# Four query loads begun by two DMA queues in place of one, in an attention kernel on one core

## The chip, the cores and the metric

The kernel runs on one core of a Trainium2 chip. The metric is the device time of one execution in microseconds (us); most runs of one kernel agree within 0.2 us. Times of kernels that were compared were taken on the same chip, in turns.

## The reference

```python
B, H, Sq, Skv, Dh = 8, 16, 16, 2048, 256      # all bfloat16, normal values times 0.05
def reference(q, k, v):
    scores = jnp.einsum('bhqd,bhkd->bhqk', q, k) * q.shape[-1] ** -0.5
    return jnp.einsum('bhqk,bhkd->bhqd', softmax(scores, axis=-1), v)
```

There are 128 heads. K and V are 134 MB each and are read once; Q is 1 MB. The inputs are so small that all softmax weights are nearly equal. The correctness check cannot tell a wrong order of the query heads.

## The kernel before

A job `J(engine, class, emit, deps, dma)` is one instruction or a few; an engine runs its jobs in the order in which they were made. SyncE ("sp") begins all loads, so they stand in one queue.

```python
ku = k.rearrange("b h s d -> (b h s) d").rearrange("(u p t) d -> u p t d", p=128, t=NT)   # 4 heads each
qx = q.rearrange("b h s d -> (b h s) d").rearrange("(u a s) d -> a u (s d)", a=4, s=SQ)
QR = VB[:, 1, 0:SQ, :].rearrange("p s d -> p (s d)")      # query rows, in V's second buffer

def emit_qload(eng, a):           # 32 heads (every fourth) to 32 partitions, 8 KB each
    return eng.dma_start(QR[32 * a:32 * a + 2 * G, :], qx[a])        # 2 * G is 32
def emit_qt(eng):                 # VectorE, 32x32 blocks
    return eng.transpose(QT[:].bitcast(F32), QR.bitcast(F32))
# ... cut ...
j_q = [J("sp", "ldq", lambda eng, a=a: emit_qload(eng, a), [j_qz], dma=(sem_q, 64)) for a in range(4)]
# ... cut: then K of the first 8 heads in four loads of 2 MB (two halves of two blocks), which wait
# for nothing; the next K loads wait for the transposes ("kt") that free their buffer; then V ...
j_qt[0] = J("dve", "qt", emit_qt, j_q)
```

After that, ScalarE spreads QT into block-diagonal weights QW, VectorE transposes K in 32x32 blocks ("kt", KN to KB), TensorE multiplies, and so on for 16 groups of 8 heads. A block of K holds four heads, one in each quadrant of 32 partitions. So query head 4u+a has to be in quadrant a, which is why the queries come in four loads of 32 partitions.

## Time and profile before

| | before |
|---|---|
| time, median of 6 runs | 639.76 us (639.58 to 639.93) |
| span of the profiled run | 638.1 us |
| bytes moved | 270.62 MB |

The page of the profile of the kernel before, its span and the rate of all DMA engines in 40 equal slices:

```profile
span 638.1 us, 5071 instructions
...
GB/s 312 429 436 429 430 429 442 429 440 427 431 427 431 429 431 431 429 435 438 426 443 427 431 427 431 429 429 433 433 431 438 438 431 427 430 427 431 420 426 265
```

The rate is about 430 GB/s in all slices but the first and the last. The view by windows gives, for stretches from the start of the span, the busy time of each engine (with instructions in brackets), the granted clock, the DMA share and the rate:

```profile
core 0: us, PE busy (x) PEld busy (x) DVE busy (x) ACT busy (x) POOL busy (x), PEclk, DMA share, GB/s
2.00:4.00 2.00, 0.00 (x0) 0.00 (x0) 0.08 (x1) 0.02 (x1) 2.00 (x1) 1.00 1.05 258
4.00:6.00 2.00, 0.00 (x0) 0.00 (x0) 0.00 (x0) 0.00 (x0) 0.92 (x1) 1.00 0.98 217
6.00:8.00 2.00, 0.00 (x0) 0.00 (x0) 0.00 (x0) 0.00 (x0) 0.00 (x0) 1.00 0.99 291
8.00:10.00 2.00, 0.00 (x0) 0.00 (x0) 0.44 (x1) 0.00 (x0) 0.00 (x0) 1.00 1.04 434
200.00:300.00 100.00, 74.55 (x310) 21.74 (x218) 69.16 (x62) 11.62 (x22) 0.00 (x0) 0.90 1.00 432
```

In the middle (200 to 300 us) the 16 DMA engines are busy all the time, at 432 GB/s. From 4 to 6 us they are just as busy (0.98), at half of that, 217 GB/s. A busy DMA engine is not a fast one. The timeline of the start says what was loaded (start, duration, engine, line, operation, and in brackets what ended the idle time before):

```profile
0.74 1.77 SPq L110 DMA_DIRECT2D VB<-in_q_dram  x4
...
2.56 16.47 SPq L212 DMA_DIRECT2D KN<-in_k_dram  x5
9.56 2.31 DVE L113 STREAM_TRANSPOSE QT<-VB 128x2048 f32<-128x2048 f32 x1 [7.48 <-DMA VB<-in_q_dram]
...
14.17 4.50 DVE L128 STREAM_TRANSPOSE KB<-KN 128x2048 f32<-128x2048 f32 x2 [2.30 <-DMA KN<-in_k_dram]
...
18.73 0.61 PE L145 MATMUL S_ps<-KB,QW 128*128 128x512 bf16 x1 [18.73 <-DVE KB L128]
```

The four query issues take 1.77 us of SyncE's time, and K's follow. QT's transpose waits for the queries until 9.56 us, but the first K transpose waits still longer, until 14.17 us. The chain of waits, followed back from the end, is here (start, duration, what):

```profile
605.20 28.28 DMA KN<-in_v_dram
...
633.52 1.93 PE O_ps L178 x16
...
635.55 0.48 DVE O_fin L326
```

The last V loads were begun at 605 us and stood 28 us in a full queue. The kernel is bound by the DMA stream from the start to the tail.

### The profile page before, as it was taken

The page shows a single profiled execution, that of the slowest core. Times are in us where ns is not written, and L with a number is a line of the kernel's source. Part 1 is how long each engine was busy: PE and PEld are TensorE (multiplying, and loading weights), DVE is VectorE, ACT ScalarE, POOL GpSimd, SP SyncE. Part 2 cuts the span into 40 slices and gives each one's busy share as a digit, 9 for nine tenths or more (in the row PEclk, how much of TensorE's full clock was granted, in tenths as well). Part 3 has the DMA queues.
Part 4 walks back from the last instruction along what each step waited for, and adds up shares of the span by engine and source line. Part 5 has one row for each costly group of instructions (what it writes and reads, how often), then busy time and mean ns, then how long its engine had stood idle before and what let it go on. Part 6 is the DMA issues. An engine that isn't in the chain of part 4 may idle for free. (4 is left out here: it accounts for less than half of the span.)

```text
span 638.1 us, 5071 instructions
## 1 busy us (share of the span) xinstructions
PE 490.0 (77%) x2176; PEld 166.1 (26%) x1680; DVE 428.2 (67%) x371; ACT 93.8 (15%) x176; POOL 4.2 (1%) x7
## 2 busy tenths in 40 slices
PE   0748959959499595986959779595995949959897
PEld 0101312314132140321303123131231412214286
DVE  3879494875948569385683957749477594766960
ACT  2030301203021030300303003030120303003010
POOL 2000000000000000000000000000000000000000
PEclk9977987979889798997979979799797989979999
DMA  8999999999999999999999999999999999999996
GB/s 312 429 436 429 430 429 442 429 440 427 431 427 431 429 431 431 429 435 438 426 443 427 431 427 431 429 429 433 433 431 438 438 431 427 430 427 431 420 426 265
DMA packets 13766, 270.62 MB, mean 424 GB/s; under 512 B 1600, under 2 KB 3904, under 8 KB 4416
## 3 DMA queue, kind: packets, MB, share of 16 engines
q1 hardware_dynamic: 13344, 270.36, 99.2%
q10 hardware_dynamic: 416, 0.18, 0.1%
q8 instruction: 4, 0.07, 0.0%
q14 instruction: 2, 0.02, 0.0%
HBM read 269.48 MB, written 1.05 MB: 424 GB/s over the span
## 5 line engine op out<-in xcount | busy, mean ns | idle before, releaser
L145 PE MATMUL S_ps<-KB,QW 128*128 128x512 bf16 x528 | 217.0, 420 | 137.2 <-DMA VB<-in_v_dram 94.1
L128 DVE STREAM_TRANSPOSE KB<-KN 128x2048 f32<-128x2048 f32 x128 | 284.7, 2281 | 55.2 <-DMA KN<-in_k_dram 53.0
L133 PE MATMUL S_ps<-KB,QW 128*128 128x512 bf16 x496 | 207.7, 419 | 0.0
L172 PE MATMUL O_ps<-VB,PT 128*128 128x512 bf16 x896 | 195.6, 379 | 6.8 <-DMA VB<-in_v_dram 6.8
L145 PEld LDWEIGHTS S_ps<-KB,QW 128*128 128x128 bf16 x528 | 54.6, 104 | 345.2 <-issue 282.5
L172 PEld LDWEIGHTS O_ps<-VB,PT 128*128 128x128 bf16 x896 | 86.8, 98 | 118.3 <-issue 15.7
L150 DVE TENSOR_REDUCE negm<-S_ps 128x1 f32<-128x2048 f32 x16 | 36.7, 2292 | 89.2 <-PE S_ps L133 89.2
L154 ACT ACTIVATE P_sb<-S_ps,negm 128x2048 bf16<-128x2048 f32 x16 | 31.5, 1967 | 414.1 <-DVE negm L150 414.1
L158 DVE STREAM_TRANSPOSE PC<-P_sb 128x1024 bf16<-128x1024 bf16 x32 | 37.9, 1222 | 33.8 <-ACT P_sb L154 33.8
L164 DVE COPY PT<-PC 32x1024 bf16<-32x1024 bf16 x128 | 53.5, 418 | 3.4 <-PE O_ps L178 1.7
L122 ACT ACTIVATE QW<-QT 32x128 bf16 (+1 forms) x128 | 54.0, 422 | 11.2 <-DVE QT L113 9.9
L315 ACT ACTIVATE O_tmp<-O_ps,rab 128x256 f32<-128x256 f32 x15 | 7.1, 475 | 93.6 <-issue 93.6
L178 PE MATMUL O_ps<-KN,PT 128*128 128x256 bf16 x128 | 14.6, 273 | 1.1 <-DMA KN<-in_v_dram 1.1
L178 PE MATMUL O_ps<-VB,PT 128*128 128x256 bf16 x128 | 14.1, 273 | 0.4 <-DVE PT L164 0.4
L178 PEld LDWEIGHTS O_ps<-KN,PT 128*128 128x128 bf16 x128 | 12.3, 98 | 3.3 <-issue 1.1
L178 PEld LDWEIGHTS O_ps<-VB,PT 128*128 128x128 bf16 x128 | 12.4, 98 | 2.3 <-DVE PT L164 0.8
L326 DVE TENSOR_SCALAR O_fin<-O_ps,rab 128x256 bf16<-128x256 f32 x2 | 1.0, 484 | 13.0 <-PE O_ps L178 7.2
L320 DVE SCALAR_TENSOR_TENSOR O_fin<-O_ps,rab,O_tmp 128x256 bf16<-128x256 f32 x15 | 6.7, 446 | 1.8 <-issue 1.8
L113 DVE STREAM_TRANSPOSE QT<-VB 128x2048 f32<-128x2048 f32 x1 | 2.3, 2311 | 7.5 <-DMA VB<-in_q_dram 7.5
L297 DVE TENSOR_SCALAR rab<-mask,rinv 128x2 f32<-128x2 f32 x16 | 3.7, 229 | 1.5
L191 POOL MEMSET PT<- 128x4096 f32 x1 | 3.5, 3511 | 0.0
L301 DVE COPY rab<-rab 128x2 f32<-128x2 f32 x15 | 2.5, 167 | 1.2
(11 smaller groups left out, 8.3 us busy)
## 6 DMA issues: line engine op xcount, KB each, us to landing
VB<-in_v_dram SPq DMA_DIRECT2D x28, 4096.0 KB, 23.9
KN<-in_k_dram SPq DMA_DIRECT2D x28, 4096.0 KB, 30.0
KN<-in_k_dram SPq DMA_DIRECT2D x8, 2048.0 KB, 15.0
VB<-in_v_dram SPq DMA_DIRECT2D x4, 2048.0 KB, 17.1
KN<-in_v_dram SPq DMA_DIRECT2D x2, 2048.0 KB, 27.7
KN<-in_v_dram SPq DMA_DIRECT2D x2, 1024.0 KB, 24.3
KN<-in_v_dram SPq DMA_DIRECT2D x3, 512.0 KB, 27.7
VB<-in_q_dram SPq DMA_DIRECT2D x4, 256.0 KB, 5.1
```

Source lines behind the costliest of these rows:

```text
L122: ins = eng.activation(ap_of(dv, dv.offset + 32 * a + e, [[256, 4], [128, 2], [2, 16]]), src.rearrange("p (s b) t -> p b t s", b=4), ACTF. ...
L128: return eng.transpose(KBf[:, c % R_KB].rearrange("p t i -> p (t i)"), KNf[:, e].rearrange("p t i -> p (t i)")[:, n * c:n * c + n])
L133: return eng.add_instruction(mybir.InstMatmult(start_tensor_calc=start, stop_tensor_calc=stop, ldweights=False, tile_size=(128, 128), tile ...
L145: ins = mm(S_ps[:, 2 * h + c, :], QW[:, e, bp, :], rhs, start=(e == 0 and bp == 0), stop=(e == 1 and bp == 7))
L150: return eng.tensor_reduce(out=negm[:], in_=S_ps[:].rearrange("p c n -> p (c n)"), axis=AX.X, op=ALU.max, negate=True)
L154: return eng.activation(P_sb[:], S_ps[:].rearrange("p c n -> p (c n)"), ACTF.Exp, bias=negm[:], scale=1.0, accum_out=lsum[:])
L158: return eng.transpose(PC[:, h].rearrange("p t x -> p (t x)"), P_sb[:, 1024 * h:1024 * h + 1024])
L164: ins = eng.tensor_copy(PT[pr, 32 * h:32 * h + 32, pr], PC[pr, h])
L172: ins = eng.matmul(O_ps[:, 0, :], PT[:, t, :], rhs, start=(t == 0), stop=(t == NT - 1))
L178: ins = eng.matmul(O_ps[:, bank, 0:D], PT[:, t, :], buf[:, t, :], start=(t == 0), stop=(t == NT - 1))
L315: j_ea[g] = J("act", "ea", lambda eng: eng.activation(O_tmp[:], src, ACTF.Copy, scale=rab[:, 0, 0:1]), [("pv", g, 1) if g < last - 1 else ...
L320: j_eb[g] = J("dve", "eb", lambda eng: eng.scalar_tensor_tensor(out=O_fin[:, 0, :], in0=src, scalar=rab[:, 0, 1:2], in1=O_tmp[:], op0=ALU. ...
```

## The change

The intent: the queries of quadrants 0 and 1 are begun by SyncE, those of 2 and 3 by ScalarE, so that each DMA engine has packets of both sorts to choose from.

```diff
-        j_q = [J("sp", "ldq", lambda eng, a=a: emit_qload(eng, a), [j_qz], dma=(sem_q, 64)) for a in range(4)]
+        j_q = [J(("sp", "sp", "act", "act")[a], "ldq", lambda eng, a=a: emit_qload(eng, a), [j_qz], dma=(sem_q, 64)) for a in range(4)]
 # ... cut: two more jobs stand at the head of ScalarE's list, so the loop's indices move by 2 ...
-                 "act": [order["act"][1:3]] + [order["act"][3 * x:3 * x + 3] for x in range(1, last)]}
-        n_tail = {"dve": dve_tail, "pe": 6 * last - 2, "act": 3 * last}
+                 "act": [order["act"][3:5]] + [order["act"][3 * x + 2:3 * x + 5] for x in range(1, last)]}
+        n_tail = {"dve": dve_tail, "pe": 6 * last - 2, "act": 3 * last + 2}
 # ... cut: bookkeeping, "jb.eng == 'sp' or jb.cls == 'st'" becomes "jb.cls in ('ld', 'ldq', 'st')" ...
```

The edit is meant to leave the waits of all engines as they were; both pages count 5071 instructions.

## The prediction

> **What bounds the kernel now.** The DMA stream. The page moves 270.62 MB in a span of 638.1 us (mean 424 GB/s); the view by windows gives a DMA share of 1.00 and 430 to 432 GB/s in every stretch from 18 to 600 us, while TensorE (77%) and VectorE (67%) wait for loads. The chain of waits ends in 28.28 us of "DMA KN<-in_v_dram": the last V loads stand in a full queue. About 431 GB/s over 270.62 MB is 628 us; the rest is start and tail. So DMA time saved at the start should arrive at the end.
>
> **Where the start loses time.** By windows, the stream begins at about 1.5 us, then runs at 180 to 260 GB/s from about 3 to 7.5 us (DMA share near 1.0, so the engines are occupied, not starved), and reaches 410 to 490 GB/s after 8 us. That is the four query loads (256 KB and 32 partitions each). Summing the windows, 2.05 MB have moved by 9.0 us; at 431 GB/s from 1.6 us this would have taken until 6.4 us. So about 2.6 us are lost, and this is the most the change can win. The Trainium skill, "SBUF — State Buffer", section "Door 1: The DMA port swizzle", says that partitions 0 to 63 reach only 8 of 16 DMA ports and 64 to 127 the other 8. The trace agrees in size: about 215 GB/s is half of 431. Loads 0 and 1 share one half, 2 and 3 the other; one queue sends them one after the other.
>
> **What the change does.** Two of the four issues (0.42 us each) move from SyncE to ScalarE, ahead of its table load (1.28 us). ScalarE then waits until 11.90 us for QT anyway, so this is free. SyncE begins its K issues some 0.85 us sooner, worth nothing by itself, since the queue is occupied. Nothing else changes. The gain is that packets for both halves are available to each DMA engine together. If ports were then all used, 1.05 MB would take 2.4 us in place of 4.8 us.
>
> **How much of it.** The same page, section "Can I just issue two DMAs to hit both halves?", reports only +6% for that, and says they serialize: each DMA engine alternates between its two queues, and two engines with the same port in step still block each other. Engines out of step by part of a packet would gain a part. Estimate: gain between 0.3 us (in step) and 2.4 us (all ports), centre 1.4 us, fully on the critical path. QT (9.56 us now) is not critical: K's first transpose waits 2.3 us longer, until 14.17 us.
>
> **Time.** 639.79 - 1.4 = 638.4 us, range 637.2 to 639.7. Faster by over 2% needs 12.8 us, five times the whole loss: 0.5%. Slower by over 2%: 0.5%. Within 2%: 99%.
>
> **What would show it.** Right: GB/s from 2 to 6 us above 260; QT's transpose at 7 to 9 us; the first K transpose at 12 to 13.6 us instead of 14.17; the same shift in the first matmul (18.73 us) and the start of the last V wait; 431 GB/s unchanged in the middle; span shorter by the same amount as the first K transpose is earlier. Wrong: if 2 to 6 us still shows about 215 GB/s, the queues stay in step and nothing is won. If the first K transpose is earlier but the end is not, a stage in the middle was not bound by DMA.
>
> **What would make it wrong.** K rows of the SyncE queue passing ScalarE's query rows, so that QT lands later than K and becomes critical; ScalarE's issues starting late; a mid-kernel stall that absorbs the shift.

## The result

| | before | after |
|---|---|---|
| time, median of 6 runs each | 639.76 us | 639.12 us (638.91 to 639.21) |
| ratio | | 0.999, 95% interval 0.9977 to 1.0003 |
| span of the profiled run | 638.1 us | 637.7 us |
| repeated later (9 and 5 runs) | 639.65 us | 639.06 us |

A ratio is the mean time of one kernel's runs over that of the other's of the same rounds, so it is not quite the ratio of these medians. The interval is wider than the effect. But all six runs after are below all six runs before, and the repetition gives the same difference: 0.64 us, then 0.59 us. I take the change to be worth about 0.6 us. That is 0.1%, and less than half of the predicted 1.4 us.

The page of the changed kernel, the same lines:

```profile
span 637.7 us, 5071 instructions
...
GB/s 311 429 443 428 426 430 440 430 438 434 432 428 432 432 428 432 430 430 430 431 443 438 432 430 429 430 432 432 428 432 430 440 432 430 432 436 430 417 423 274
```

By windows, the same stretches:

```profile
2.00:4.00 2.00, 0.00 (x0) 0.00 (x0) 0.07 (x1) 0.95 (x1) 2.00 (x1) 1.00 0.90 258
4.00:6.00 2.00, 0.00 (x0) 0.00 (x0) 0.00 (x0) 0.00 (x0) 0.91 (x1) 1.00 1.05 246
6.00:8.00 2.00, 0.00 (x0) 0.00 (x0) 0.00 (x0) 0.00 (x0) 0.00 (x0) 1.00 1.01 299
8.00:10.00 2.00, 0.00 (x0) 0.00 (x0) 0.28 (x1) 0.00 (x0) 0.00 (x0) 1.00 1.03 418
200.00:300.00 100.00, 74.69 (x314) 21.81 (x221) 69.00 (x62) 11.60 (x22) 0.00 (x0) 0.90 1.00 432
```

From 4 to 6 us the rate rose from 217 to 246 GB/s, where all ports would have given 430; from 2 to 4 us it did not rise, and from 8 to 10 us it is lower than before. A second profile of the same kernel (the run "The change once more" below) shows a faster start:

```profile
2.00:6.00 4.00, 0.00 (x0) 0.00 (x0) 0.07 (x1) 0.96 (x1) 2.91 (x1) 1.00 1.01 277
4.00:6.00 2.00, 0.00 (x0) 0.00 (x0) 0.00 (x0) 0.00 (x0) 0.91 (x1) 1.00 1.19 291
```

So from 4 to 6 us the two profiles of one kernel (246 and 291 GB/s) lie further apart than the first of them and the kernel before. Over 2 to 6 us it is 238 GB/s before, and 252 and 277 after. The timeline of the first profile's start:

```profile
0.73 0.86 SPq L110 DMA_DIRECT2D VB<-in_q_dram  x2
0.73 0.90 ACTq L110 DMA_DIRECT2D VB<-in_q_dram  x2
...
1.64 17.24 SPq L212 DMA_DIRECT2D KN<-in_k_dram  x5
...
9.72 2.31 DVE L113 STREAM_TRANSPOSE QT<-VB 128x2048 f32<-128x2048 f32 x1 [7.65 <-DMA VB<-in_q_dram]
...
14.01 4.50 DVE L128 STREAM_TRANSPOSE KB<-KN 128x2048 f32<-128x2048 f32 x2 [1.98 <-DMA KN<-in_k_dram]
...
18.58 0.61 PE L145 MATMUL S_ps<-KB,QW 128*128 128x512 bf16 x1 [18.58 <-DVE KB L128]
```

The issues ran side by side, as intended (0.86 and 0.90 us), and K's issues began at 1.64 us in place of 2.56. But QT's transpose began a little later than before (9.72), and the first K transpose 0.16 us earlier (14.01). In the second profile of the same kernel it was 0.49 us earlier (13.68). The end of the chain of waits:

```profile
593.87 30.26 DMA KN<-in_v_dram
624.27 10.79 PE O_ps L178 x96
635.15 0.48 DVE O_fin L326
```

The last wait for V now ends at 624 us; the 96 matmuls after it run without a gap, where by its chain the kernel before still waited for V until 633.5 us.

Why was so little won? The DMA view of the changed kernel shows a part of it. These are four stretches of 0.5 us in order, 3.5 to 5.5 us. q1 is SyncE's queue, q10 is ScalarE's; columns are packets, MB, and the share of the 16 engines' time:

```profile
q10 hardware_dynamic: 15, 0.08, 63.5%
q1 hardware_dynamic: 12, 0.04, 32.3%
...
q1 hardware_dynamic: 23, 0.12, 98.3%
q10 hardware_dynamic: 10, 0.00, 2.0%
...
q1 hardware_dynamic: 10, 0.08, 69.2%
q10 hardware_dynamic: 6, 0.05, 45.1%
...
q10 hardware_dynamic: 12, 0.10, 84.2%
q1 hardware_dynamic: 2, 0.00, 0.4%
```

In the first and the last stretch the engines work mostly for ScalarE's queue, in the second nearly only for SyncE's (98% against 2%). The records of single packets, from which these shares are made, show rows of both queues mixed at 3.1 us (8 and 8 under way), then turns: 15 of SyncE's and none of ScalarE's at 4.4 us, none and 16 at 5.5 us, 16 and none at 6.6 us. So most of the 16 engines turn from one queue to the other together. By theory, while all write quadrants 0 and 1 the ports of the other half have nothing to do, and the other way round, and this keeps the gain small. The turns are seen in the trace; this consequence is argued, and the packets support it only weakly. Rows that had 4 to 7 others of their own queue beside them, and as many of the other queue, still took 463 ns; those with 10 or more of their own took 527 (second profile: 448 and 460).

The packets also give the size. A query row of 8 KB took 563 ns on average before; after, 521 on SyncE's queue and 504 on ScalarE's (493 over both in the second profile). In the wide load below the mean is 363 ns and the median 309. So the change took away some 50 to 70 of 200 ns, and with 8 rows for each engine that is 0.4 to 0.6 us. About half of it was lost again on K's rows of 16 KB: those begun before 17 us took 645 ns on average before, 657 and 663 in the two profiles after, and 611 in the kernel with the wide load. With 268 rows over 16 engines this is 0.2 to 0.3 us.

### The profile page after: what moved, and what is told of

Its sections match the earlier page's. It is cut to its first block, busy times and chain, and to the rows that moved or that the text cites. A ratio compares the mean times of both kernels' runs of the same rounds, so it can differ in the third digit from the quotient of the medians.

```text
span 637.7 us, 5071 instructions
## 1 busy us (share of the span) xinstructions
PE 485.4 (76%) x2176; PEld 165.5 (26%) x1680; DVE 428.3 (67%) x371; ACT 93.8 (15%) x176; POOL 4.2 (1%) x7
## 3 DMA queue, kind: packets, MB, share of 16 engines
HBM read 269.48 MB, written 1.05 MB: 424 GB/s over the span
## 4 chain that ended last, share of the span: by engine, by line
DMA 72%; DVE 18%; issue 5%; PE 4%; ACT 0%; SPq 0%; DVEq 0%; ACTq 0%
DMA KN<-in_k_dram 67%; DVE KB L128 17%; DMA KN<-in_v_dram 5%; PE O_ps L178 2%; PE S_ps L145 1%; PE S_ps L133 1%; DVE negm L150 0%; ACT QW L122 0%; SPq L110 0%; DVE O_fin L326 0%; SPq L230 0%; DVEq L481 0%; ACT P_sb L154 0%; ACTq L122 0%; ACTq L484 0%
## 5 line engine op out<-in xcount | busy, mean ns | idle before, releaser
L145 PE MATMUL S_ps<-KB,QW 128*128 128x512 bf16 x528 | 214.3, 414 | 138.3 <-DMA VB<-in_v_dram 95.0
L133 PE MATMUL S_ps<-KB,QW 128*128 128x512 bf16 x496 | 204.8, 413 | 0.0
```

The lines of the kernel that those rows point to most:

```text
L133: return eng.add_instruction(mybir.InstMatmult(start_tensor_calc=start, stop_tensor_calc=stop, ldweights=False, tile_size=(128, 128), tile ...
L145: ins = mm(S_ps[:, 2 * h + c, :], QW[:, e, bp, :], rhs, start=(e == 0 and bp == 0), stop=(e == 1 and bp == 7))
```

## The experiments

The theory A: a load of 32 partitions reaches half of the ports. The Trainium skill, "SBUF — State Buffer", section "Door 1: The DMA port swizzle", puts partitions 0 to 63 on 8 ports and 64 to 127 on the other 8. The engines then work through the two halves in step (T). Rivals: the first microseconds are slow whatever is loaded (C), the source pattern in HBM is slow (B), a second queue as such is what won 0.6 us (Q). A theory about the end, S: the slowest of the 16 DMA engines sets it, not their mean.

The trace records when each of the 16 engines completes a load, but not which engine it was. For K's first half load (2 MB, the first load after the queries), in us (the names below `after, again` are the labels of runs that follow: two queues with the same half, narrow loads from consecutive heads and on every fourth partition, four wide loads, one wide load, one wide load with the right order):

```
kernel          median engine   last engine   span     span - last
before              12.28          14.07      638.1      624.0
after               12.32          13.92      637.7      623.8
after, again        12.17          13.59      637.6      624.0
same_half           12.44          13.99      638.1      624.1
narrow_dense        12.45          14.20      638.3      624.1
stride4             12.69          14.33      638.5      624.2
wide_four           11.68          13.21      637.3      624.1
wide_one            10.29          11.87      635.5      623.6
wide_perm           10.34          11.89      635.5      623.6
```

From the last engine's arrival at the first K load, the end follows 623.6 to 624.2 us later. So what is decided in the first 14 us stays to the end, but only to within 0.6 us, and the change won no more than that. The traces show what blurs it. Near 3.5, 593, 615 and 630 us, in most of these kernels, a packet of 16 KB of kind "instruction" (queue q8 of the page) occupies a DMA engine, for 1.05 to 1.18 us in the kernel before and for 1.70 us at the start of the changed one. The first of these seems to be what makes one engine late: in `wide_perm` it comes at 9.39 us (1.01 us long), there the 16 engines end the query load within 0.5 us of each other, and a lag of 1.55 us first appears at K's first load. Later the lag of the last engine behind the median jumps when another such packet comes, but not in every profile: at 630 us in the kernel before (from 1.79 to 2.46 us), at 593 us in the second profile of the changed kernel (from 1.46 to 2.15 us).

### The change once more

No edit.

> The changed kernel unedited, for a second profile and a tighter interval. Theory A (32-partition loads reach half of the DMA ports, and the 16 DMA engines walk through the two halves in step): 250 GB/s between 3.5 and 6.5 us again, the median engine ends K's first half load no earlier than in the kernel before (12.3 us), the last engine 0.1 to 0.2 us earlier (13.9). If the 0.64 us of the first measurement is real: 639.1 us, with the kernel before at 639.8. If the 0.3 us won in the tail (last V piece 634.41 against 634.86 us) is chance of where an instruction fetch falls, this second profile shows another tail.

Measured: 639.06 us against 639.65, ratio 0.9993 (0.9979 to 1.0006). From 4 to 5 us the windows show 254 GB/s. The median engine came 0.11 us earlier than before, the last engine 0.48. So the gain was repeated (span 0.5 us shorter). The way to it is not straight, though. The last engine was 0.48 us earlier at the first K load, and 0.15 us in the first profile. At 619 us, after the instruction packets near 593 us, it was 0.02 us earlier in this profile and 0.11 us later in the first one; at the last V load, after the jump of the kernel before at 630 us, 0.60 and 0.45 us earlier. Single profiles can't tell how much of the 0.6 us was won at the start.

### A wide query load

```diff
-        j_q = [J("sp", "ldq", lambda eng, a=a: emit_qload(eng, a), [j_qz], dma=(sem_q, 64)) for a in range(4)]
+        j_q = [J("sp", "ldq", lambda eng: eng.dma_start(QR[:, :],
+               q.rearrange("b h s d -> (b h) (s d)")), [j_qz], dma=(sem_q, 16))]
```

> Wrong result on purpose: one query load of 128 partitions from consecutive rows, so heads are in the wrong order; bytes are the same. Theory A (ports): 400 GB/s or more from 2.5 us on, the query load complete by about 5.5 us, K's first half load at the median engine at about 10.0 us in place of 12.3, the whole kernel 2 to 3 us faster (637 us). Rival C (the first microseconds are slow whatever is loaded): 215 to 250 GB/s until 7 us again, K's first half at 12.3 us, time unchanged.

Measured: 636.92 us against 639.65, ratio 0.9958 (0.9944 to 0.9972): 2.73 us faster. The windows show 410 GB/s from 3 to 4 us. This run changes the width of the load and the number of loads at once, which a later run takes up. C falls. Of the 2.73 us, 2.2 are there at the last engine of K's first load and stay until 629 us; the rest comes from 630 us on, where the kernel before has its jump. The packets account for the 2.6 us that the prediction counted as "the most the change can win": in the kernel before, the time of query rows over 309 ns and of K's rows (begun before 17 us) over 611 ns adds up to 2.0 and 0.6 us for each engine; here it is 0.4 us in all. (The heads are in the wrong order; see the remark at the reference.)

### Narrow loads from consecutive heads

```diff
-    qx = q.rearrange("b h s d -> (b h s) d").rearrange("(u a s) d -> a u (s d)", a=4, s=SQ)
+    qx = q.rearrange("b h s d -> (b h s) d").rearrange("(a u s) d -> a u (s d)", a=4, s=SQ)
```

> Wrong result on purpose: four query loads of 32 partitions on one queue as before, but each reads 32 consecutive heads (256 KB in one piece) in place of every fourth. Theory A (ports): 215 GB/s until 6 us, as before, K's first half at the median engine at 12.3 us, time 639.8 us. Rival B (the source's stride of 32 KB in HBM is what is slow): 350 GB/s or more, K's first half at about 10 us, 2 us faster.

Measured: 639.48 us against 639.65, ratio 0.9996 (0.9981 to 1.0012); 221 GB/s from 3 to 5 us and 213 from 5 to 6. B falls: the stride in HBM is not what is slow.

### K's first half before the queries

```diff
                 for h in range(2):
+                    if (u, h) == (0, 1):
+                        q_load()          # the four query jobs, on SyncE, made here
                     j_k[u, h] = J("sp", "ld", ...
```

> Correct result: K's first half load (128 partitions, 2 MB) is begun before the four query loads, all on SyncE. Theory A (ports): the first 2 MB move at 400 GB/s or more from about 2.5 us, K's first half at the median engine at about 7.2 us, and then the queries at about 215 GB/s until about 11.7 us; the loss is only moved, so the second K half ends at the median engine at 17.2 us as before. Rival C (slow start whatever is loaded): 215 to 250 GB/s until 7 us, then the queries at 400. Theory S (the slowest engine, held up by the instruction fetch at 3.2 us among half-rate rows, decides the end): its lag of 1.8 us behind the median is smaller here, and the time up to 0.6 us shorter.

Measured: 641.20 us against 639.65, ratio 1.0022 (1.0008 to 1.0035): slower by 1.55 us. The windows of this kernel, 2 to 10 us:

```profile
2.00:4.00 2.00, 0.00 (x0) 0.00 (x0) 0.07 (x1) 0.02 (x1) 2.00 (x1) 1.00 0.76 270
4.00:6.00 2.00, 0.00 (x0) 0.00 (x0) 0.00 (x0) 0.00 (x0) 0.91 (x1) 1.00 0.98 410
6.00:8.00 2.00, 0.00 (x0) 0.00 (x0) 0.00 (x0) 0.00 (x0) 0.00 (x0) 1.00 1.03 401
8.00:10.00 2.00, 0.00 (x0) 0.00 (x0) 0.00 (x0) 0.00 (x0) 0.00 (x0) 1.00 0.94 197
```

The wide load runs at about 400 GB/s, and the slow stretch is now at 8 to 10 us, where the queries are (197). This again speaks for A and against C. The time went against every theory named. The loss was not only moved: K's second half load ended at the median engine at 18.16 us, not 17.2, and at the last one at 20.73 us (18.98 before), so the lag that S expected to shrink grew to 2.57 us. QT's transpose began at 16.17 us and the first K transpose at 18.41 us, so the jobs that free buffers came late. The V loads issued at 81.91 us before were now issued at 85.36 us. From 80 to 96 us the stream ran at 393 GB/s in place of 440: the queue had run short. Over these 16 us that is 47/440 of 16, about 1.7 us. This looks like the cause of the slower time, but the arrivals say that it is not. At the median engine, loads were 0.96 us late against the kernel before until 85 us and 2.26 us from 95 us on: here the shortage is seen. At the last engine they were 1.76 us late already at K's second half load, and still 1.75 us at 95 us and 1.73 at 593. The 1.55 us are the last engine's, so they were lost in the first 21 us, and the shortage at 80 us cost the end nothing. Why this start loses 1.8 us more, in place of moving its loss, stays open.

### Two queues that hold the same half

```diff
-        j_q = [J(("sp", "sp", "act", "act")[a], ...
+        j_q = [J(("sp", "act", "sp", "act")[a], ...
```

> Correct result: two queues as in the change, but paired otherwise: SyncE begins query loads 0 and 2, ScalarE 1 and 3, so that both queues hold the same half of the ports at any time (0 with 1, then 2 with 3). Theory A (the 0.6 us of the change come from packets of both halves being on the way together): 215 GB/s from 3.5 to 6 us, K's first half load at the last engine at 14.1 us, time 639.7 us, no gain over the kernel before. Rival Q (the gain comes from having a second queue, whatever it holds): 639.1 us, as the change.

Measured: 639.79 us against 639.78, ratio 1.0000 (0.9986 to 1.0014). Nothing is won, and from 4 to 6 us the windows show 229 GB/s. The query rows took 572 ns on average, no less than the 563 of the kernel before, where the change brought 512. Q falls: the 0.6 us of the change come with both halves being on the way together, not with a second queue. The issues stand on the same two engines as in the change, so another layout of the program is not what won them either. (The two kernels were each measured against the kernel before, on different chips, not against each other.)

### Narrow loads on every fourth partition

```diff
-            return eng.dma_start(QR[32 * a:32 * a + 2 * G, :], qx[a])
+            return eng.dma_start(QR[a:128:4, :], qx[a])
```

> Wrong result on purpose: four query loads of 32 partitions on one queue as before, but load a goes to partitions a, a+4, a+8 and so on[...] (heads end up in the wrong order). Theory T (the engines walk in step: each writes two rows of a load, and at each row two engines meet at one port and half of the ports stand idle): 215 to 280 GB/s from 3.5 to 6 us, K's first half at the median engine at 11.7 to 12.3 us, time 639.2 to 639.8 us. Rival P (what counts is how many ports a load reaches in all): 400 GB/s, K's first half at 10.3 us, time 637 us.

Measured: 640.32 us against 639.78, ratio 1.0013 (0.9997 to 1.0028), with a wide spread (639.83 to 641.05). Each load now has partitions of both halves. The time decides nothing: SyncE needed 3.61 us to issue these four loads in place of 1.78 (one issue took 1.71 us, the others 0.57 to 0.60), so the engines stood idle around 4 us (DMA share 0.52 from 4 to 5 us) and K's loads began late. The packets say more. The query rows took 397 ns on average and 309 in the median, as in the wide load, also where 14 or more of them were under way together (77 rows, median 309). As far as the rows go this speaks for P and against T.

### Four wide loads of a quarter each

```diff
+        j_q = [J("sp", "ldq", lambda eng, a=a: eng.dma_start(QR[:, 1024 * a:1024 * a + 1024],
+               q.rearrange("b h s d -> (b h) (s d)")[:, 1024 * a:1024 * a + 1024]), [j_qz], dma=(sem_q, 64)) for a in range(4)]
```

> Wrong result on purpose: four query loads of 256 KB on one queue, each of all 128 partitions and a quarter of the columns (2 KB rows). Theory A (ports): 400 GB/s, K's first half at the median engine at about 10.3 us, time 637 us, as with one wide load. Rival D (what made the single wide load fast is one completion in place of four, or a load of 1 MB in place of 256 KB): about 250 GB/s, K's first half at about 12 us, time above 639 us.

Measured: runs of 638.76 to 640.30 us, median 639.37, ratio 0.9999 (0.9984 to 1.0015). A miss for both. The windows show 283 GB/s from 3 to 4 us and 176 from 4 to 5, now with a DMA share below 1 (0.93 and 0.83): the small loads left engines without work, a loss of another kind than the 16 busy engines of the narrow loads. So wide loads alone are not enough; this one, of 2 KB rows and with four completions, is not fast either. How much of that is the row and how much the number of loads stays open, and so does whether one load in place of four is a part of what the single wide load won. That narrow loads as such are slow rests on their rows: 16 busy engines with 563 ns a row, where the wide load's median is 309 ns, and on the same-half pairing.

### Queries on one queue, K at once on the other

```diff
-        j_q = [J(("sp", "sp", "act", "act")[a], ...
+        j_q = [J("act", ...                        # and the indices of ScalarE's loop by 2 more
```

> Correct result: ScalarE begins all four query loads, and SyncE begins K's loads at once, so that each DMA engine alternates between a query row (8 KB, half of the ports) and a K row (16 KB, all ports). Theory T (the 16 engines turn from one queue to the other in step): a query row still takes about 0.6 us and a K row 0.61, so the loss is the same 8 x 0.3 us, only spread until about 11.5 us: K's second half load at the median engine at about 17.2 us, time 639.5 to 640.5 us. Rival P (with both queues full, some engines write K rows while others write query rows, and the ports stay busy): 350 GB/s or more from 3 to 10 us, K's second half at 15.5 us, time 637.5 us.

Measured: 641.81 us against 639.49, ratio 1.0043 (1.0030 to 1.0057), slower by 2.3 us. P falls: the rate from 3 to 11 us is 312 GB/s, and the records show most engines turning from K rows to query rows and back together (16 and none under way at 3.8 us, 4 and 11 at 4.4, 15 and none at 5.2). T's direction holds, but not its sizes: query rows took 400 ns on average in place of its 600, K's rows begun before 17 us 840 in place of 610, and the median engine ended K's second half load at 18.57 us, 1.4 us later than before. The last engine was 1.84 us late there and 2.2 us from 47 us on. So most of the 2.3 us was lost at the start; the 0.4 us after 40 us may come from the late start of compute (QT's transpose began at 18.45 us).

### More work for 8 of the 16 DMA engines

```diff
+            if g == 4:
+                for x in range(4):
+                    j_st["x", x] = J("sp", "ld", lambda eng, x=x: eng.dma_start(XS[8 * x:8 * x + 8, :],
+                        q.rearrange("b h s d -> (b h) (s d)")[8 * x:8 * x + 8, 0:2048]), dma=(...))
```

> Correct result: the kernel before with four more loads of 8 partitions and 4 KB rows in mid-kernel, which go to 8 of the 16 DMA engines (0.6 us of work for each of those at the 27 GB/s of one engine seen here), into a buffer that nobody reads. Theory S (the end is set by the one engine that is 1.7 to 2.0 us behind the median): if that engine is not among the 8, the end does not move (639.7 us) although 8 engines have 0.6 us more; if it is, the end moves by 0.6 us (640.3) and the last engine's lag grows to 2.4 us. Rival M (the mean of the engines counts): half of 0.6 us, 640.0 us.

Measured: 640.13 us against 639.49, ratio 1.0010 (0.9997 to 1.0024). Not usable as a test: the trace shows all 16 engines delayed, the first by 0.8 us too, although it should have lost nothing. Eight neighbouring partitions may themselves be a narrow target: in the next run, which differs in this alone, the first engine lost only 0.06 us. Repeated with the 8 rows spread over partitions 4 apart (`XS[x:32:4, :]`):

> Correct result: as the run with four extra loads of 8 partitions before, which went to 8 neighbouring partitions[...] and delayed all engines (first engine +0.8 us, median +1.2, last +0.6 us): [...]only the 8 engines that carry them should lose time, 0.6 us each. Theory S (one late engine sets the end): 639.6 us if that engine is not among the 8, 640.2 if it is, and the first or the median engine moves by at most 0.6 us. Rival M (the mean counts): 639.9 us.

Measured: 639.71 us against 639.74, ratio 1.0001 (0.9987 to 1.0014). In the first K load after the extra ones, the median engine came at 173.65 us (173.16 before) and stayed about 0.5 us late, the last engine at 174.98 us (174.96 before). Half of the engines got 0.5 us more to do and the end did not move. The time alone would not tell S from M (639.6 from 639.9 us, with an interval of 0.9 us to each side). The arrivals support S, but not cleanly: until 583 us the last engine kept its time of the kernel before to 0.03 us, then it lost 0.8 us at 593 us, where the kernel before lost 0.6 us at 630. Two other runs are clearer. At 593 us, with K first and with the queries on their own queue, the last engine was 1.73 and 2.25 us late and the median 2.25 and 2.76; the times were 1.55 and 2.32 us longer, as the last engine says. That it is one and the same engine from 14 to 583 us is inferred from its lag, which stays at 1.8 to 1.9 us in the kernel before.

### A wide load and the right order

To have the wide load and a correct result, the rows must change places on chip. TensorE was idle at the start, so it does this, with a permutation matrix `PM` (1 where p = 4u + a):

```diff
+        j_pmz = J("pool", "pmz", lambda eng: eng.memset(PM[:], 0.0))
+        j_pm = J("pool", "pm", lambda eng: eng.affine_select(out=PM[:].rearrange("p (a u) -> p a u", a=4), in_=...,
+            compare_op=ALU.not_equal, fill=1.0, base=0, pattern=[[-1, 4], [-4, 32]], channel_multiplier=1), [j_pmz])
+        # one wide query load, as above; 8 matmuls of 512 columns into 8 PSUM banks:
+        #   eng.matmul((S_ps if y < 4 else O_ps)[:, y % 4, :], PM[:], QR[:, 512 * y:512 * y + 512], start=True, stop=True)
+        # 4 copies of two banks each to QP, two by VectorE and two by ScalarE; QT is made from QP
```

> Correct result, meant to beat both kernels: one query load of 128 partitions in memory order; TensorE brings the rows to their quadrants by eight matmuls with a 128x128 permutation matrix, VectorE and ScalarE copy the eight PSUM banks back to SBUF (two copies each), then everything as before. Theory A and a start that is bound by DMA alone: K's first half at the last engine at 11.9 us and the end as in the wide load with wrong order, 636.9 us, although QT comes 2 to 4 us later than there (about 12 us in place of 7.1) and the first score matmul at about 18 us in place of 16.5. If compute at the start does count: up to 1.5 us more, 638.4 us.

Measured: 636.99 us against 639.78, ratio 0.9957 (0.9943 to 0.9970): 2.79 us faster than the kernel before, and by the two differences (2.79 and 0.6) about 2.2 us faster than the change. Each of its five runs (636.85 to 637.05) is below each run of both. The windows of this kernel:

```profile
2.00:4.00 2.00, 0.00 (x0) 0.00 (x0) 0.07 (x1) 0.00 (x0) 2.00 (x2) 1.00 0.74 303
4.00:6.00 2.00, 0.29 (x1) 0.14 (x2) 0.00 (x0) 0.00 (x0) 1.52 (x1) 1.00 1.10 467
6.00:8.00 2.00, 2.00 (x6) 0.76 (x5) 1.17 (x1) 0.34 (x1) 0.00 (x0) 1.00 0.92 393
8.00:10.00 2.00, 1.28 (x4) 0.15 (x1) 1.28 (x2) 1.99 (x3) 0.00 (x0) 1.00 1.08 459
200.00:300.00 100.00, 74.00 (x309) 21.70 (x219) 67.47 (x62) 11.61 (x22) 0.00 (x0) 0.90 1.01 433
```

From 4 to 6 us it moves 467 GB/s where the kernel before moved 217 (a short window takes a whole packet at its end, so values over 432 are no rate that lasts). The timeline of its start:

```profile
0.74 0.38 SPq L202 DMA_DIRECT2D VB<-in_q_dram  x1
...
5.71 1.87 PE L208 MATMUL S_ps<-VB,PM 128*128 128x512 bf16 x4 [5.71 <-DMA VB<-in_q_dram]
...
11.03 2.31 DVE L115 STREAM_TRANSPOSE QT<-VB 128x2048 f32<-128x2048 f32 x1 [1.27 <-ACT VB L214]
13.26 6.66 DVE L130 STREAM_TRANSPOSE KB<-KN 128x2048 f32<-128x2048 f32 x3
...
17.78 0.61 PE L147 MATMUL S_ps<-KB,QW 128*128 128x512 bf16 x1 [8.50 <-DVE KB L130]
```

QT comes at 11.03 us, later than in any kernel above with the queries first, and the first K transpose has to wait for it, until 13.26 us. It costs nothing: the time is that of the wide load with the wrong order (636.92). The start is bound by DMA, with some microseconds of slack for compute. That the order is right was not shown by the correctness check. It can be read from the program: `PM` has a single 1 in each column, so that row 32a + u of the product is query head 4u + a, as the four loads of the kernel before place it. No run here tests it with inputs that would show an error.

## Why the prediction was right or wrong

The time (639.12 us) is in the range, 637.2 to 639.7, and "within 2%" was right. The gain was over-estimated: 1.4 us said, about 0.6 us measured.

- **"What bounds the kernel now. The DMA stream."** Right. 432 GB/s in the middle, before and after.
- **"About 2.6 us are lost, and this is the most the change can win."** Right in size: the packets of the kernel before add up to 2.6 us for each engine. That the wide load won 2.73 us and the corrected one 2.79 is in part luck, since at the start they won 2.2 us and the rest at 630 us.
- **Half of the ports.** Right as far as rates can show it: narrow loads from consecutive heads stayed at 213 to 221 GB/s, the wide load reached 410, and two queues that hold the same half won nothing.
- **The issues: "this is free" and K's earlier issue "worth nothing by itself".** Right. The same-half pairing has the same issues and the same time as before.
- **"Estimate: gain between 0.3 us (in step) and 2.4 us (all ports), centre 1.4 us."** This is the term that was mis-sized. The mechanism was named, but I put the centre halfway. The DMA view shows the engines nearly in step (98% against 2% in one stretch); a query row took 521 and 504 ns in place of 563, where the wide load has 363, and K's rows after it took back about half of what this won. The gain belonged near the lower end. Why mixed rows were no faster is not shown.
- **"GB/s from 2 to 6 us above 260; QT's transpose at 7 to 9 us; the first K transpose at 12 to 13.6 us."** In the first profile all three failed: 252 GB/s, 9.72 us, 14.01 us. In the second the rate held (277 GB/s), and the other two failed more narrowly (9.39 and 13.68 us). The span was to become shorter by as much as the first K transpose came earlier: 0.4 us against 0.16, then 0.5 us against 0.49.
- **"QT ... is not critical."** Right; in the last version it is 1.5 us later than before and the kernel faster. In the run with K first, with QT 6.6 us later, the queue did run short at 80 us, which cost the median engine 1.3 us and the last one nothing.
- **What the prediction left out.** It spoke of the rate of all engines together. What counts is the last engine: the median engine's arrival at the first K load did not change (12.28, then 12.32 and 12.17 us), the last engine's did (14.07, then 13.92 and 13.59).

What stays open: why the engines fall into step so closely (their turns are seen; no run broke the step without changing something else); why K's first rows are slow for 2 us after the queries in both kernels (the 8 to 10 us window of the changed kernel is below that of the kernel before); and how much of the 0.6 us is won at the start and how much depends on where the instruction packets near 593 and 630 us fall (the last engine's lead at the first K load is 0.15 us in one profile and 0.48 in the other).

## What to carry to other kernels

When the DMA engines are busy at half of the rate that the same kernel reaches elsewhere, ask which partitions the load writes, and make the load wide before trying to overlap narrow ones: two queues with opposite halves won 0.6 us here, one wide load and a shuffle on an idle engine 2.8 us. In a kernel that is bound by DMA from start to end, read when the last of the 16 engines completes a load, not the mean: half of the engines had 0.5 us to spare at no cost. And check that a test could see the error you risk, here the order of the heads.

## What the Trainium skill lacked or had wrong

- "SBUF — State Buffer", section "Door 1: The DMA port swizzle": agrees. 32-partition loads ran at 213 to 221 GB/s against 432 GB/s for 128 partitions.
- The same page, section "Can I just issue two DMAs to hit both halves?", says they serialize, at +6%. Near the truth here: from 2 to 6 us, 252 and 277 GB/s in two profiles against 238 (+6% and +16%). It does not tell what the trace shows, that most engines turn from queue to queue together, nor how to make one wide load of rows that must go to given quadrants: here a shuffle on chip after it won 2.79 us.
- "DMA: Bandwidth & Descriptors", section "Issuing engines are not separate DMA queues", says that a second issuing engine only saves issue time. Pairing decides here: with both halves mixed 0.6 us were won, with the same half on both queues none.
- No page that I read says how long the issue takes for a stepped destination. A load of 32 partitions took SyncE 0.38 to 0.42 us at step 1 and 0.57 to 0.60 us at step 4, where one of the four took 1.71 us.
- No page that I read says that an engine that falls behind at the start stays behind for the whole kernel: 1.80 us behind the median at 14 us, and still 1.84 us at 594 us (592.51 and 594.35). Nor does one say that a 16 KB instruction packet takes 1.0 to 1.7 us of a DMA engine that carries the kernel's loads; the lag after it was 1.4 to 1.8 us.
